# The memory read-out of an attention kernel done head by head: two 64-row matmuls into two PSUM banks in place of one 128-row matmul

## The chip, the core and the metric

The program runs on one core of one Trainium2 chip. The metric is the time of one execution on the device, in microseconds (us); lower is better. The chip's engines run side by side, each with its own queue of instructions in program order: TensorE (PE: weight loads, called PEld in the trace, and matmuls), VectorE (DVE), ScalarE (ACT), GpSimd (POOL) and SyncE (SP), which only issues transfers here.

## The reference

Four batches, eight heads, 576 tokens and head size 64 go through causal softmax attention mixed with a compressive memory, then through two MLPs (512 to 2048 to 512):

```python
B, H, S, D = q.shape                      # 4, 8, 576, 64
a = softmax(causal(q @ k.T / sqrt(D)))
local = a @ v
q_p = elu(q) + 1
mem_ret  = einsum('bhsd,bhde->bhse', q_p, M_prev)
mem_norm = einsum('bhsd,bhd->bhs', q_p, z_prev)[..., None] + 1e-06
g = sigmoid(beta)
x = g * mem_ret / mem_norm + (1 - g) * local    # (tokens, 512)
x = silu(x @ w_in) @ w_out                      # first MLP
h = x @ w_in2;  out = (h * tanh(softplus(h))) @ w_out2
```

The change is in how `mem_ret` and `mem_norm` reach the mix.

## The kernel before

Heads are taken in pairs: head 0 of a pair lies on partitions 0 to 63, head 1 on partitions 64 to 127 (16 pairs). A step is one block of up to 128 queries of one pair: first 32 steps with query blocks 0 and 1 of all pairs, then 48 with blocks 2, 3 and 4 (block 4 has 64 queries), 80 steps in all. Each step goes through three stages:

- `stage_a` makes the scores of both heads in two PSUM banks, the softmax numerators as two f16 parts (high and low), and sends them through a transposing DMA. For the blocks 0 and 1 the scores are f32 matmuls on 64 rows (partitions), one for each head; then masks are added by a matmul with the identity on 128 rows.
- `stage_b` is the read-out. On PE it multiplies the transposed numerators by v, three f16 matmuls for each head and key block (65, 64 and 65 columns; column 65 of v is ones and gives the softmax denominator). Then comes one f32 matmul for the memory: the features of both heads (`er`, 128 rows) against a block-diagonal matrix `rm` of 128 rows and 130 columns, in which each head has its 64 columns of M_prev, one of z_prev, and zeros in the other head's rows. After the last step of a pair of query blocks (or after block 4) DVE adds the small constants to the denominators, takes reciprocals, multiplies by the gates (`gvv`) and by the numerators (`t4`), and POOL adds memory and local part (`x`).
- `stage_c` transposes `x` on PE (line 610), ACT or DVE copies it out of PSUM (`xo`), and SP stores it to the scratch tensor `xd` in DRAM, from which `chunk_x` loads the MLP's inputs, 256 tokens at a time.

The mix of a pair of query blocks lies in banks 6 and 7: an even block in bank 6, an odd one in bank 7, each with columns 0 to 64 for the local part of head 0, 65 to 129 for that of head 1, and 130 to 259 for the memory of both. The transposes of `stage_c` go to columns 260 and up of the same two banks.

All instructions are handed to a planner (`Plan`) as operations with a priority, the regions that they write and read, and a cost formula. `issue` then runs a list scheduler over all engines and so fixes the order of every queue before the program is built. Regions are kept as one interval of bytes: a strided view that spans banks 6 and 7 counts as everything from its first to its last byte. Attention has a higher priority than the MLP's matmuls (`gemm1`, `gemm2`), which fill PE in between. On PE a line number says little, since nearly all matmuls are issued by the helper `mm` (line 375); `tt` is line 328, `stt` 322, `ts` 319, `act` and `copy` on ACT 314, and DMAs are line 385.

In the first part of the program the first MLP's weights are unpacked (`weight_unit`, 16 units), measured (`weight_scale`, once for the first eight units, which are w_in, and once for the last eight, w_out) and split into two f16 parts (`weight_split`) on ACT and DVE, while attention runs beside it. `hidden` of the first MLP needs the scale of w_out as well. Matmul outputs of `gemm1` go to banks 2 and 3 in turn, so the third group of eight (`gemm1` of step 2) waits until `hidden` of step 0 has read bank 2.

Of the kernel before, what the change touches and what calls it, by code (L numbers as in the profile page):

```python
# [9 lines left out]
F32 = mybir.dt.float32  # L10
F32R = mybir.dt.float32r
U32 = mybir.dt.uint32
# [3 lines left out]
ALU = mybir.AluOpType  # L16
# [16 lines left out]
PT_BLOCKS = 50  # L33
VM = 130 + NQ * 2 * (D + 1)
COLD = 50000.
# [143 lines left out]
def attn_moe_moe2_kernel(ctx: ExitStack, tc: tile.TileContext, kq, vm, beta, w1, w2, out):  # L179
# [92 lines left out]
    pt_tile, = carve([PT_BLOCKS, 128], F16)  # L272
    kqr, rmr, rvr = ring(carve([2, S], F32, 2)), ring(carve([130], F32, 3)), ring(carve([VM - 130], F32, 2))
    khr, klr = ring(carve([S], F32R, 2)), ring(carve([S], F32R, 2))
# [119 lines left out]
    def setup():  # L394
# [9 lines left out]
        def consts():  # L404
# [7 lines left out]
            make_identity(nc, ident)  # L412
            nc.gpsimd.memset(eps[:, 0:2], 1e-9 * PSCALE)
            nc.gpsimd.memset(eps[:, 2:4], 1e-6)
            nc.gpsimd.memset(ones, 1.0)
            nc.gpsimd.memset(onesf, 1.0)
            for t in scales:
                nc.gpsimd.memset(t[:, 2:4], 1.0)
            for t in v1s:
# [4 lines left out]
        g3 = gb.rearrange("p (a h) -> p a h", h=2)  # L424
        ts(p, gv[:, :, 0:2], g3, -0.5, ALU.mult, 0.5, ALU.add)
        ts(p, gv[:, :, 2:4], g3, 0.5, ALU.mult, 0.5, ALU.add)

# [15 lines left out]
    def load_vm(v, prio):  # L443
        p, _, nk = VISITS[v]
        n = nk * 2 * (D + 1)
        t, rm[v] = rvr()[:, 0:n], rmr()
        rv[v] = t.rearrange("p (n e d) -> p n e d", n=nk, e=2)
        dma(prio, t, vm[p, :, 130:130 + n], reads=[])
        dma(prio, rm[v], vm[p, :, 0:130], reads=[])

# [23 lines left out]
    def prep_v(v, prio):  # L474
# [7 lines left out]
        mm(prio, [(total, ones, top, True, True)])  # L482
        ts(prio, inv[:, 0:2], total.to_broadcast([128, 2]), 2.0**-14, ALU.mult, 1e-30, ALU.max)
        ts(prio, inv[:, 0:2].bitcast(U32), inv[:, 0:2].bitcast(U32), 0x7F800000, ALU.bitwise_and)
        other(prio, "DVE", 160, lambda: nc.vector.reciprocal(out=scale, in_=inv[:, 0:1]), [scale], [inv])
# [80 lines left out]
    def stage_b(n, prio):  # L566
# [4 lines left out]
        v1, v2, gvv = vv[v]  # L571
        vb = bank[6 + qt % 2]
        if qt < 4:
# [16 lines left out]
        g = banks[0:R, 512 * 6:512 * 8].rearrange("p (b c) -> p b c", b=2)[:, 0:m, 0:260].rearrange("p b (a c) -> p b a c", a=4)  # L590
        den, t4, x = denr()[0:R, 0:m], t4r()[0:R, 0:m], xr()[0:R, 0:m]
        each = lambda y: y[0:R].unsqueeze(1).to_broadcast([R, m, 4])
        tt(prio, den, g[:, :, :, D], each(eps), ALU.add)
        other(prio, "DVE", 165, lambda: nc.vector.reciprocal(out=den, in_=den), [den], [den])
        tt(prio, den, den, each(gvv), ALU.mult)
        tt(prio, t4, g[:, :, :, 0:D], den.unsqueeze(3).to_broadcast([R, m, 4, D]), ALU.mult)
        tt(prio, x, t4[:, :, 0:2], t4[:, :, 2:4], ALU.add, ("POOL", "DVE"))
        xts[n] = (x, R)
# [319 lines left out]
```

## Time and profile before

| | |
|---|---|
| median of 3 runs | 1025.33 us (1025.13 to 1026.48) |
| the profiled execution: its own time | 1025.4 us |
| its span (first to last instruction) | 1023.6 us |
| PE matmuls busy | 948.2 us, 93% of the span |
| DVE, ACT, POOL busy | 673.4, 642.5, 273.9 us |
| TensorE's granted clock, mean over the span | 0.96 |

The profiled execution takes 1.8 us more than its span, and lies 0.1 us above the median of the runs. Busy times of engines overlap. A PE row's duration holds a fixed latency, so matmuls that follow each other overlap in it; what a matmul costs in a full queue is the distance between its start and the start of the next one.

### The profile page before, as it was taken

To read this page: it belongs to the slowest core of one execution; us is meant where nothing else is said; L and a number is where in the kernel's file an instruction comes from. 1 tells how busy PE (TensorE), PEld (TensorE's weight loads), DVE (VectorE), ACT (ScalarE), POOL (GpSimd) and SP (SyncE) were. 2 spreads that over 40 slices of the span, in tenths; PEclk is the share of its full clock that TensorE was granted. 3 is DMA by queue.
4 is the path that set the end of the run, shared out by engine and by line. 5 is a ranking of instruction groups with operands and counts; after the bars stand their busy time and mean duration, and the time that the engine had idled before them with its cause. 6 is when DMAs were issued, how large, how long until landed. Compare 5 with 4: busy or idle time off the path is not lost.

```text
span 1023.6 us, 20794 instructions
## 1 busy us (share of the span) xinstructions
PE 948.2 (93%) x8364; PEld 732.2 (72%) x8364; DVE 673.4 (66%) x1231; ACT 642.5 (63%) x1095; POOL 273.9 (27%) x280
## 2 busy tenths in 40 slices
PE   2436589999999999999999999999999999999998
PEld 1225478888888888888888888766676766766665
DVE  6988687787787878777757756754544545544433
ACT  7977665666666756756667676744555545555544
POOL 1110123343343433432322522212212122222221
PEclk9956589999999999999999999999999999999999
DMA  9767924775787767845353341100100101000000
GB/s 322 230 148 208 228 58 114 162 187 133 183 156 150 151 137 148 176 114 130 105 199 104 104 146 61 42 30 14 42 22 21 32 12 42 22 21 22 1 21 21
DMA packets 149904, 107.93 MB, mean 105 GB/s; under 512 B 111152, under 2 KB 139312, under 8 KB 145712
## 3 DMA queue, kind: packets, MB, share of 16 engines
q1 hardware_dynamic: 149664, 106.60, 40.1%
q8 instruction: 65, 1.06, 0.4%
q14 instruction: 31, 0.25, 0.1%
q10 hardware_dynamic: 144, 0.00, 0.0%
HBM read 66.21 MB, written 14.16 MB: 79 GB/s over the span
## 4 chain that ended last, share of the span: by engine, by line
PE 85%; DMA 6%; DVE 4%; ACT 4%; issue 1%; SPq 0%; POOL 0%; DVEq 0%; POOLq 0%; ACTq 0%
PE banks L375 84%; DMA arena<-arena 2%; DVE w L322 1%; PE banks L610 1%; DMA g<-w 1%; ACT w L314 1%; DMA xs<-xd 1%; ACT arena L314 1%; DMA ws<-w 1%; DVE arena L322 1%; DMA arena<-kq 1%; ACT ws L671 0%; DVE w L328 0%; DVE arena L328 0%; DMA arena<-vm 0%
## 5 line engine op out<-in xcount | busy, mean ns | idle before, releaser
L375 PEld LDWEIGHTS <-w 128*128 128x128 f16 x3456 | 334.8, 98 | 43.3 <-issue 4.2
L375 PEld LDWEIGHTS <-arena 128*128 128x128 f16 (+1 forms) x3168 | 225.5, 101 | 80.1 <-DMA arena<-arena 27.5
L328 POOL TENSOR_TENSOR g<-ga,g 128x512 f16<-128x512 f32 x108 | 144.1, 1335 | 345.7 <-ACT g L314 327.4
L375 PE MATMUL banks<-xh,w 128*128 128x256 f16 x1728 | 213.8, 275 | 2.6 <-DVE ga L322 2.6
L375 PE MATMUL banks<-g,w 128*128 128x256 f16 x1728 | 209.8, 273 | 0.1
L375 PE MATMUL banks<-xh,arena 128*128 128x256 f16 x1728 | 198.6, 273 | 0.0
L375 PE MATMUL banks<-arena,g 128*128 128x512 f16 x864 | 197.4, 379 | 0.0
L375 PE MATMUL banks<-arena 128*128 128x65 f16 (+6 forms) x1728 | 119.0, 235 | 62.1 <-DMA arena<-arena 24.1
L375 PEld LDWEIGHTS <-g 128*128 128x128 f16 x864 | 84.5, 98 | 87.6
L314 ACT ACTIVATE ga<-ga 128x512 f32<-128x512 f32 x108 | 67.6, 628 | 77.5 <-DVE ga L319 53.6
L314 ACT ACTIVATE arena<-arena 128x256 f32<-128x256 f32 (+6 forms) x180 | 101.5, 592 | 18.5 <-PE banks L375 9.5
L322 DVE SCALAR_TENSOR_TENSOR ga<-ga,banks 128x512 f32<-128x512 f32 x108 | 73.7, 683 | 54.2 <-ACT ga L314 53.7
L322 DVE SCALAR_TENSOR_TENSOR arena<-arena 128x256 f16<-128x256 f32 (+6 forms) x144 | 106.1, 746 | 3.9 <-ACT arena L314 3.4
L314 ACT ACTIVATE w<-w 128x512 f32<-128x512 f32 x108 | 66.6, 625 | 47.3 <-DVE w L319 26.3
L314 ACT ACTIVATE arena<-banks,arena 128x128 f32<-128x128 f32 (+4 forms) x144 | 73.9, 545 | 33.9 <-DVE arena L546 25.9
L314 ACT ACTIVATE g<-ga 128x512 f16<-128x512 f32 x106 | 66.3, 626 | 28.7 <-DVE ga L322 28.2
L328 POOL TENSOR_TENSOR arena<-arena 128x256 f32<-128x256 f32 (+1 forms) x48 | 44.0, 916 | 139.1 <-DVE arena L328 89.3
L314 ACT ACTIVATE ga<-banks,xsc 128x512 f32<-128x512 f32 x72 | 49.2, 685 | 49.2 <-PE banks L375 45.5
L546 DVE TENSOR_REDUCE arena<-banks 128x2 f32<-128x256 f32 (+3 forms) x80 | 64.3, 804 | 23.8 <-PE banks L375 19.9
L328 POOL TENSOR_TENSOR g<-w,g 128x512 f16<-128x512 f32 x36 | 41.6, 1156 | 126.2 <-ACT g L314 126.2
L375 PEld LDWEIGHTS banks<-arena 128*128 128x128 f32 (+2 forms) x288 | 42.4, 228 | 32.9 <-ACT arena L314 29.6
L319 DVE TENSOR_SCALAR ga<-banks,xsc 128x512 f32<-128x512 f32 x36 | 27.0, 750 | 51.7 <-PE banks L375 51.6
(95 smaller groups left out, 942.0 us busy)
## 6 DMA issues: line engine op xcount, KB each, us to landing
ws<-w SPq DMA_DIRECT2D x28, 1024.0 KB, 5.3
arena<-kq SPq DMA_DIRECT2D x16, 576.0 KB, 5.0
arena<-vm SPq DMA_DIRECT2D x16, 325.0 KB, 3.4
xs<-xd SPq DMA_DIRECT2D x9, 512.0 KB, 4.6
yd<-w SPq DMA_DIRECT2D x36, 128.0 KB, 1.9
xs<-yd SPq DMA_DIRECT2D x9, 512.0 KB, 3.8
arena<-kq SPq DMA_DIRECT2D x16, 256.0 KB, 3.4
xd<-arena SPq DMA_DIRECT2D x32, 128.0 KB, 2.5
```

The costliest lines, as they stand in the source:

```text
L314: return ("ACT", ns, lambda: nc.scalar.activation(out=out, in_=in_, func=func, scale=scale, bias=bias))
L319: return ("DVE", ns, lambda: nc.vector.tensor_scalar(out=out, in0=in0, scalar1=s1, scalar2=s2, op0=op0, **kw))
L322: return ("DVE", 1.04 * cols(out) + 160, lambda: nc.vector.scalar_tensor_tensor(out=out, in0=in0, scalar=s, in1=in1, op0=op0, op1=op1))
L328: return (e, ns, lambda: eng.tensor_tensor(out=out, in0=in0, in1=in1, op=op))
L375: nc.tensor.matmul(out=o, lhsT=l, rhs=r, start=a, stop=z)
L546: other(prio, "DVE", 1.04 * cols(both) + 146, lambda: nc.vector.tensor_reduce(out=m1, in_=both, axis=AX, op=ALU.max, negate=True), [m1], [ ...
L610: plan.add(prio, [("PE", 56, lambda o=o, x2=x2: nc.tensor.transpose(o, x2, ident[0:R, 0:R]))], [o], [x2, ident], edge=(107, 56))
```

## The change

`rm` holds 65 columns in place of 130: for each partition the 64 values of its own head's M_prev and one of z_prev, without the zeros. The memory part becomes two f32 matmuls, one for each head, on that head's 64 partitions and with 65 columns. The mix is laid out by head: head 0 in bank 6, head 1 in bank 7, an even query block at columns 0 to 129 and an odd one at 130 to 259, each with 65 columns of the local part and then 65 of the memory. The constants, gates and the tiles of the mix change their order to match; the number of their instructions and elements stays. The planner and its cost formulas stay.

```diff
-VM = 130 + NQ * 2 * (D + 1)
+VM = D + 1 + NQ * 2 * (D + 1)
...
-        dma(prio, rm[v], vm[p, :, 0:130], reads=[])
+        dma(prio, rm[v], vm[p, :, 0:D + 1], reads=[])
...
-        vb = bank[6 + qt % 2]
+        c0 = 130 * (qt % 2)
...
-            o = vb[0:R, 65 * e:65 * e + 65]
+            o = bank[6 + e][0:R, c0:c0 + 65]
...
-        mm(prio, ms + [(vb[0:R, 130:260], er[v][:, 128 * qt:128 * qt + R], rm[v], True, True)])
+        for e in range(2):
+            r = slice(64 * e, 64 * e + 64)
+            ms.append((bank[6 + e][0:R, c0 + 65:c0 + 130], er[v][r, 128 * qt:128 * qt + R], rm[v][r], True, True))
+        mm(prio, ms)
...
-        g = banks[0:R, 512 * 6:512 * 8].rearrange("p (b c) -> p b c", b=2)[:, 0:m, 0:260].rearrange("p b (a c) -> p b a c", a=4)
+        g = banks[0:R, 512 * 6:512 * 8].rearrange("p (e c) -> p e c", e=2)[:, :, 0:130 * m].rearrange("p e (a c) -> p e a c", c=65)
...
-        tt(prio, x, t4[:, :, 0:2], t4[:, :, 2:4], ALU.add, ("POOL", "DVE"))
+        t4 = t4.rearrange("p e (q k) d -> p e q k d", k=2)
+        tt(prio, x.rearrange("p q e d -> p e q d"), t4[:, :, :, 0], t4[:, :, :, 1], ALU.add, ("POOL", "DVE"))
...
-    mz = np.zeros((NP, 2, D, 2, D + 1), f32)
-    for e in range(2):
-        mz[:, e, :, e, :D] = np.asarray(M_prev).reshape(NP, 2, D, D)[:, e]
-        mz[:, e, :, e, D] = np.asarray(z_prev).reshape(NP, 2, D)[:, e]
+    mz = np.concatenate([np.asarray(M_prev).reshape(NP, 128, D), np.asarray(z_prev).reshape(NP, 128, 1)], 2)
```

Since each step now writes both banks, the planner orders all queues differently from the first read-outs on. Three places follow.

The first is PE, at the read-outs of the steps 2 and 3 (an even and an odd block). "128x130" is the memory matmul before; a "128x65" without a LDWEIGHTS row ahead of it is one of the two after (an f32 matmul loads its own weights). L610 (L616 after) are the transposes of `stage_c` of the pair ahead of it, diag the matmul of `weight_scale`. Before:

```order
L375 MATMUL banks<-arena_98 128x65
L375 MATMUL banks<-arena_98 128x130 [waits DMAHW2_49]
L610 MATMUL banks<-ident_66,arena_98 128x128 [waits Pool_49]
L610 MATMUL banks<-ident_66,arena_98 128x128
L375 MATMUL banks<-diag_81,onesf_96 128x128 [waits DVE_49]
L375 LDWEIGHTS arena_98 [waits DMAHW2_49]
L375 MATMUL banks<-arena_98 128x65 [waits Activation_49]
```

After:

```order
L616 MATMUL banks<-ident_66,arena_98 128x128 [waits Pool_49]
L616 MATMUL banks<-ident_66,arena_98 128x128
L375 MATMUL banks<-diag_81,onesf_96 128x128 [waits DVE_49]
L375 LDWEIGHTS arena_98 [waits DMAHW0_49]
L375 MATMUL banks<-arena_98 128x65 [waits Activation_49]
...
L375 MATMUL banks<-arena_98 128x65
L375 MATMUL banks<-arena_98 128x65 [waits DMAHW2_49]
L375 MATMUL banks<-arena_98 128x65
```

Before, the even block's read-out (first two rows) stood ahead of the transposes and only the odd block's waited for ACT, which copies the transposes out of PSUM; after, the even block's read-out stands behind them and has that wait.

The second place is PE just ahead of `gemm1` of step 2 (the first `xh_75,w_73` row). L610 and L616 are `stage_c` of the pair of steps 14 and 15, the `ones` matmul is `prep_v`'s, 128x256 with the two masks is `stage_a` of step 19. Before, with the read-out of step 16 just above the first row:

```order
L375 MATMUL banks<-arena_98 128x130
L610 MATMUL banks<-ident_66,arena_98 128x128 x2
L375 LDWEIGHTS ones_72
L375 MATMUL banks<-arena_98,ones_72 128x1
L375 MATMUL banks<-arena_98 128x256 x2
L375 LDWEIGHTS ident_0_67
L375 MATMUL banks<-mask_68,ident_0_67 128x128
...
L375 LDWEIGHTS w_73
L375 MATMUL banks<-xh_75,w_73 128x256
```

After:

```order
L375 LDWEIGHTS ones_72
L375 MATMUL banks<-arena_98,ones_72 128x1
L616 MATMUL banks<-ident_66,arena_98 128x128 x2
L375 LDWEIGHTS w_73
L375 MATMUL banks<-xh_75,w_73 128x256
...
L375 MATMUL banks<-xh_75,w_73 128x256
L375 LDWEIGHTS arena_98
L375 MATMUL banks<-arena_98 128x65
```

The read-out of step 16 and the scores of step 19 have moved from ahead of this group of `gemm1` to behind it.

The third place is DVE, between the scale of w_out (`wsc`, `cvec`) and the first `hidden` (the row with `ga_79`). The `xsc` row makes the factor that `hidden` needs; `banks,arena` 128x512 is the `t4` product of steps 14 and 15; L546 and L479 are reductions of `stage_a` and `prep_v`. Before:

```order
L328 TENSOR_TENSOR arena_98<-banks,arena_98 128x512
...
L322 SCALAR_TENSOR_TENSOR arena_98<-arena_98 128x256
L641 RECIPROCAL wsc_0_92<-cvec_0_94 128x1
L546 TENSOR_REDUCE arena_98<-banks 128x2
L479 TENSOR_REDUCE arena_98<-arena_98 128x1
...
L322 SCALAR_TENSOR_TENSOR arena_98<-arena_98 128x256
L328 TENSOR_TENSOR xsc_89<-cvec_0_94,xsc_89 128x2
...
L546 TENSOR_REDUCE arena_98<-banks 128x2
L322 SCALAR_TENSOR_TENSOR w_73<-w_73,wsc_0_92 128x1024
L322 SCALAR_TENSOR_TENSOR ga_79<-ga_79,banks 128x512
```

After:

```order
L328 TENSOR_TENSOR arena_98<-banks,eps_71 128x8
...
L647 RECIPROCAL wsc_0_92<-cvec_0_94 128x1
L328 TENSOR_TENSOR cvec_0_94<-cvec_0_94 128x1
L319 TENSOR_SCALAR wsc_0_92<-wsc_0_92 128x1
L328 TENSOR_TENSOR xsc_89<-cvec_0_94,xsc_89 128x2
L328 TENSOR_TENSOR arena_98<-banks,arena_98 128x512
L322 SCALAR_TENSOR_TENSOR arena_98<-arena_98 128x256
L546 TENSOR_REDUCE arena_98<-banks 128x2
L319 TENSOR_SCALAR arena_98<-banks 128x2
L322 SCALAR_TENSOR_TENSOR w_73<-w_73,wsc_0_92 128x1024
L322 SCALAR_TENSOR_TENSOR ga_79<-ga_79,banks 128x512
```

The `t4` product, a split of `prep_v`, two reductions and one more operation have moved from ahead of the `xsc` row to behind it or further down, and the reduction over the scores of step 19, the last one ahead of the weight split before, stands there no longer.

## Rows read from the trace of the kernel before

**Rows 1.** Busy time, share of the span and instructions of each engine.

```profile
PE 948.2 (93%) x8364; PEld 732.2 (72%) x8364; DVE 673.4 (66%) x1231; ACT 642.5 (63%) x1095; POOL 273.9 (27%) x280
```

**Rows 2.** Windows: stretch, length, busy time by engine, PE clock, DMA share, GB/s.

```profile
core 0: us, PE busy (x) PEld busy (x) DVE busy (x) ACT busy (x) POOL busy (x), PEclk, DMA share, GB/s
0.00:131.50 131.50, 62.02 (x385) 41.95 (x386) 106.43 (x228) 102.22 (x181) 14.27 (x41) 0.71 0.77 224
131.50:1023.60 892.10, 886.19 (x7979) 690.26 (x7978) 566.98 (x1005) 540.33 (x915) 259.62 (x239) 1.00 0.35 88
```

**Rows 3.** Memory matmuls by shape after 131.5: count, busy us, mean ns, idle.

```profile
L375 PE MATMUL banks<-arena 128*128 128x130 f32 x94 | 22.0, 315 | 0.0
...
L375 PE MATMUL banks<-arena 128*64 128x130 f32 x32 | 6.6, 288 | 0.0
```

**Rows 4.** Timeline, PE: memory matmul of 128 queries, then of 64 (start, us).

```profile
187.60 0.47 PE L375 MATMUL banks<-arena 128*128 128x130 f32 x2
187.91 0.27 PE L375 MATMUL banks<-xh,w 128*128 128x256 f16 x1
...
249.09 0.41 PE L375 MATMUL banks<-arena 128*64 128x130 f32 x2
249.44 0.28 PE L375 MATMUL banks<-xh,w 128*128 128x256 f16 x1
```

**Rows 5.** Timeline, PE: twelve MLP matmuls in a row.

```profile
312.83 1.48 PE L375 MATMUL banks<-xh,w 128*128 128x256 f16 x12
```

**Rows 6.** Timeline, PE: 64-row f32 scores, with what precedes and follows.

```profile
184.05 0.27 PE L375 MATMUL banks<-g,w 128*128 128x256 f16 x1
184.25 0.38 PE L375 MATMUL banks<-arena 64*128 64x128 f32 x2
...
184.47 0.28 PE L375 MATMUL banks<-arena 64*128 64x128 f32 x2
184.68 0.23 PE L375 MATMUL banks<-mask,ident 128*128 128x128 bf16 x1
...
172.07 0.38 PE L375 MATMUL banks<-arena 64*128 64x256 f32 x2
172.39 0.23 PE L375 MATMUL banks<-mask,ident 128*128 128x128 bf16 x1
```

**Rows 7.** Timeline, weight loads of the scores' second pass at 184 us.

```profile
184.36 0.19 PEld L375 LDWEIGHTS banks<-arena 64*128 64x128 f32 x2
```

**Rows 8.** Timeline, PE: the wait ahead of step 2's matmuls; two moved stages.

```profile
131.59 0.80 PE L375 MATMUL banks<-xh,w 128*128 128x256 f16 x3 [2.65 <-DVE ga L322]
...
156.28 0.65 PE L375 MATMUL banks<-arena 128*128 128x65 f16 x8
156.77 0.82 PE L375 MATMUL banks<-g,w 128*128 128x256 f16 x6
...
154.21 0.70 PE L375 MATMUL banks<-arena 64*128 64x256 f32 x4
```

**Rows 9.** Timeline, DVE, from the scale of w_out to the first split.

```profile
124.99 0.69 DVE L328 TENSOR_TENSOR arena<-banks,arena 128x512 f32<-128x512 f32 x1
...
125.65 0.48 DVE L322 SCALAR_TENSOR_TENSOR arena<-arena 128x256 f16<-128x256 f32 x1
...
126.44 0.41 DVE L479 TENSOR_REDUCE arena<-arena 128x1 bf16<-128x256 f32 x1
...
126.89 0.42 DVE L322 SCALAR_TENSOR_TENSOR arena<-arena 128x256 f32<-128x256 f32 x1
...
129.06 0.69 DVE L546 TENSOR_REDUCE arena<-banks 128x2 f32<-128x512 f32 x1 [1.16 <-PE banks L375]
```

**Rows 10.** Timeline, PE: the read-out of step 4, an even block.

```profile
48.08 1.08 PE L375 MATMUL banks<-arena 128*128 128x65 f16 x8 [2.46 <-DVE arena L328]
```

**Rows 11.** Timeline, SP: store of x, load of the first MLP inputs.

```profile
75.69 0.53 SPq L385 DMA_DIRECT2D xd<-arena  x1
79.75 0.39 SPq L385 DMA_DIRECT2D xs<-xd  x1
```

**Rows 12.** Waits of PE in the first 131.5 us: total, times, longest.

```profile
PE banks L375 <- DMA arena<-arena: 24.1, 4, 12.5
```

More of the change, by code (lines that the diff above doesn't have):

```diff
@@ L412, in consts @@
             make_identity(nc, ident)
-            nc.gpsimd.memset(eps[:, 0:2], 1e-9 * PSCALE)
-            nc.gpsimd.memset(eps[:, 2:4], 1e-6)
+            nc.gpsimd.memset(eps[:, 0:4:2], 1e-9 * PSCALE)
+            nc.gpsimd.memset(eps[:, 1:4:2], 1e-6)
             nc.gpsimd.memset(ones, 1.0)
@@ L417, in consts @@
             for t in scales:
-                nc.gpsimd.memset(t[:, 2:4], 1.0)
+                nc.gpsimd.memset(t[:, 1:4:2], 1.0)
             for t in v1s:
@@ L424, in setup @@
         g3 = gb.rearrange("p (a h) -> p a h", h=2)
-        ts(p, gv[:, :, 0:2], g3, -0.5, ALU.mult, 0.5, ALU.add)
-        ts(p, gv[:, :, 2:4], g3, 0.5, ALU.mult, 0.5, ALU.add)
+        ts(p, gv[:, :, 0:4:2], g3, -0.5, ALU.mult, 0.5, ALU.add)
+        ts(p, gv[:, :, 1:4:2], g3, 0.5, ALU.mult, 0.5, ALU.add)
     rq, rk, rv, rm, kk, vv, qq, er = {}, {}, {}, {}, {}, {}, {}, {}
@@ L447, in load_vm @@
         rv[v] = t.rearrange("p (n e d) -> p n e d", n=nk, e=2)
-        dma(prio, t, vm[p, :, 130:130 + n], reads=[])
-        dma(prio, rm[v], vm[p, :, 0:130], reads=[])
+        dma(prio, t, vm[p, :, D + 1:D + 1 + n], reads=[])
+        dma(prio, rm[v], vm[p, :, 0:D + 1], reads=[])
     def prep_q(v, j, prio):
@@ L482, in prep_v @@
         mm(prio, [(total, ones, top, True, True)])
-        ts(prio, inv[:, 0:2], total.to_broadcast([128, 2]), 2.0**-14, ALU.mult, 1e-30, ALU.max)
-        ts(prio, inv[:, 0:2].bitcast(U32), inv[:, 0:2].bitcast(U32), 0x7F800000, ALU.bitwise_and)
+        ts(prio, inv[:, 0:4:2], total.to_broadcast([128, 2]), 2.0**-14, ALU.mult, 1e-30, ALU.max)
+        ts(prio, inv[:, 0:4:2].bitcast(U32), inv[:, 0:4:2].bitcast(U32), 0x7F800000, ALU.bitwise_and)
         other(prio, "DVE", 160, lambda: nc.vector.reciprocal(out=scale, in_=inv[:, 0:1]), [scale], [inv])
@@ L589, in stage_b @@
         m = 1 + qt % 2
-        g = banks[0:R, 512 * 6:512 * 8].rearrange("p (b c) -> p b c", b=2)[:, 0:m, 0:260].rearrange("p b (a c) -> p b a c", a=4)
-        den, t4, x = denr()[0:R, 0:m], t4r()[0:R, 0:m], xr()[0:R, 0:m]
-        each = lambda y: y[0:R].unsqueeze(1).to_broadcast([R, m, 4])
-        tt(prio, den, g[:, :, :, D], each(eps), ALU.add)
+        g = banks[0:R, 512 * 6:512 * 8].rearrange("p (e c) -> p e c", e=2)[:, :, 0:130 * m].rearrange("p e (a c) -> p e a c", c=65)
+        den, t4, x = denr()[0:R, :, 0:2 * m], t4r()[0:R, :, 0:2 * m], xr()[0:R, 0:m]
+        quad = lambda y: y.rearrange("p e (q k) -> p e q k", k=2)
+        each = lambda y: y[0:R].rearrange("p (e k) -> p e k", e=2).unsqueeze(2).to_broadcast([R, 2, m, 2])
+        tt(prio, quad(den), quad(g[:, :, :, D]), each(eps), ALU.add)
         other(prio, "DVE", 165, lambda: nc.vector.reciprocal(out=den, in_=den), [den], [den])
-        tt(prio, den, den, each(gvv), ALU.mult)
-        tt(prio, t4, g[:, :, :, 0:D], den.unsqueeze(3).to_broadcast([R, m, 4, D]), ALU.mult)
-        tt(prio, x, t4[:, :, 0:2], t4[:, :, 2:4], ALU.add, ("POOL", "DVE"))
+        tt(prio, quad(den), quad(den), each(gvv), ALU.mult)
+        tt(prio, t4, g[:, :, :, 0:D], den.unsqueeze(3).to_broadcast([R, 2, 2 * m, D]), ALU.mult)
+        t4 = t4.rearrange("p e (q k) d -> p e q k d", k=2)
+        tt(prio, x.rearrange("p q e d -> p e q d"), t4[:, :, :, 0], t4[:, :, :, 1], ALU.add, ("POOL", "DVE"))
         xts[n] = (x, R)
@@ L903 @@
         "kq": np.concatenate([pair_t(np.asarray(k)), pair_t(np.asarray(q))], 2),
-        "vm": np.concatenate([mz.reshape(NP, 128, 130), vp.reshape(NP, 128, NQ * 2 * (D + 1))], 2),
+        "vm": np.concatenate([mz, vp.reshape(NP, 128, NQ * 2 * (D + 1))], 2),
         "betar": np.ascontiguousarray(np.broadcast_to(np.asarray(beta), (128, H))),
```

2 lines of the change are left out of this document (1 added, 1 removed).

## The prediction

> **What bounds the kernel now.** The page's first part says that PE is busy for 93% of the span [rows 1], but that is an average over two stages, so I looked at windows next. In the first 131.5 us PE works for 62.0 us at a mean granted clock of 0.71, and DVE and ACT, which unpack weights and do the softmax, for 106.4 and 102.2; from 131.5 to the end PE is busy for 886.2 of 892.1 us at full clock [rows 2]. So there are two currencies. After 131.5 every nanosecond that PE's queue gains or loses is a nanosecond of the result, and nothing else matters as long as PE isn't made to wait. Before 131.5 PE's own time is nearly free, and what counts is when the queue becomes full for good, which the first wait on the list of PE's waits (24.1 us on transposing DMAs, the longest 12.5) shows to be a matter of chains through several engines [rows 12].
>
> The boundary itself is one wait: PE reaches `gemm1` of step 2 and stands for 2.65 us until DVE has done `hidden` of step 0 [rows 8].
>
> **The memory matmul, full steps.** An f32 matmul makes two passes, each with its own weight load. Before, from the start of the first pass to the start of the next instruction, it holds PE for 187.60 to 187.91 = 0.31 us [rows 4]. Two 64-row f32 matmuls on different banks stand in this trace already: the scores of blocks 0 and 1. They show four things.
> - Entry. In a row of MLP matmuls starts are (1.48 - 0.27) / 11 = 0.11 us apart [rows 5]; from such a matmul to the first 64-row one it is 184.05 to 184.25 = 0.20 [rows 6]. Going over to 64 rows costs 0.09: PE empties first.
> - Overlap. The first passes of both heads are two rows in 0.38 us, about the length of one, so the heads do run side by side (some 0.01 apart) [rows 6].
> - Pass. First to second pass is 184.25 to 184.47 = 0.21 to 0.22, with 128 columns [rows 6].
> - Exit. From the second pass to the next 128-row instruction it is 0.21 with 128 columns and 0.32 with 256 [rows 6]: 0.11 for each 128 columns and 0.10 besides. With 65 columns that makes 0.05 + 0.10 = 0.15.
>
> What no row shows is the pass with 65 columns. If columns paced it, it would shrink to 0.05 + 0.10 = 0.16. If the weight loads pace it, it stays at 0.21, since the weights are still 128 query columns. The loads of the second pass begin at 184.36, 0.11 after the first, and their matmul starts 0.11 after that [rows 6, 7]: at 128 columns load and columns take equally long, so the load alone is enough to hold the pass at 0.21. I take 0.21 and keep 0.16 as the lower end.
>
> The Trainium skill (TensorE: Matmul & The Clock Gate, the section on LDWEIGHTS) says that a weight load's time goes with its columns and not with its rows, about 107 ns for 128 columns; as an estimate by it, two loads make a pass of 0.214 us. The 0.11 between the loads agrees, and it speaks against this change: half the rows, and no shorter load.
>
> After: 0.09 + 0.21 + 0.01 + 0.15 = 0.46 us, against 0.31: +0.15 a step (+0.10 at the lower end). Of the f32 rows 94 lie after 131.5, two passes each, so 47 steps [rows 3]; step 16 comes to them (below): 48 x 0.15 = **+7.2 us** (lower end +4.8). The order of the changed kernel's PE has a 64-row stretch of scores directly behind a read-out in four places only, and often the next read-out's 128-row f16 matmuls directly behind one, so nearly each pays both ways.
>
> **The memory matmul, block 4.** There are 16 (32 rows [rows 3]). Before, 249.09 to 249.44 = 0.35 [rows 4], in which PE already goes over from 64 output columns back to 128. After, there is one more change of shape ahead of it (0 to 0.09), the load has 64 columns, so the pass shrinks to between 0.10 and 0.21, and the exit is 0.15: 0.26 to 0.46, or -0.09 to +0.11 a step, -1.4 to +1.8 in all. With 0.09, 0.10 and 0.15 and the 0.01 it is 0.35: **0**.
>
> **Moved into the full stretch.** The read-out of step 16 (0.49 at full clock, 156.28 to 156.77) and the scores of step 19 (0.70) [rows 8] did their work on PE inside the wait for `hidden`; now they stand behind `gemm1` of step 2, which waits at the head of the queue. **+1.2 us**.
>
> **The boundary comes earlier.** The row of DVE that ends the wait stands behind the first split of w_out. Ahead of that split, three operations leave: a reduction of 0.41, a `prep_phi` operation of 0.42, and the reduction over the scores of step 19, 0.69, for which DVE had first waited 1.16 on PE [rows 9]. The other moves there are within the stretch (the `t4` product of 0.69 and the 0.48 of `prep_v` go behind the `xsc` row, so ACT can start its tanh sooner). 0.41 + 0.42 + 1.16 + 0.69 = **-2.7 us**; if ACT is late instead, 0.
>
> **Earlier waits.** An even block's read-out now stands behind the transposes of the pair ahead and waits for their copy on ACT; its 1.08 us at half clock [rows 10] no longer lies in that wait but ahead of the odd block's. The first MLP input needs three such pairs (steps 2 to 7): 0 to +3.2. Against it, SP stores x at 75.69 and then stands until 79.75, when it may load the first MLP input, 4.06 us in which nothing behind it goes out [rows 11]; in the new order two loads and a transposing DMA have moved into that gap. 0 to -4.1. The two have no row that nets them, and I take **0**.
>
> **Costs taken as nothing.** The DVE operations of the mix keep their counts and elements, and DVE has 566.98 us of work in the 892 [rows 2]; POOL's addition gets shorter inner runs, and POOL works 259.62 us there. Their results are wanted only by transposes that stand further back in PE's queue; if one were late, PE's whole queue would stand behind that transpose. The loads of `rm` stay as many, with half the bytes, in a stretch where DMA queues are busy 0.35.
>
> **Sum.** 7.2 + 0 + 1.2 - 2.7 + 0 = +5.7 on the profiled execution's 1025.4 (span 1023.6, and 0.1 over the median of the runs): **1031.1 us**. Of this kernel about 0.2%, 2.05 us, can be told from no change, so "same" is 1023.3 to 1027.4.
>
> **Rivals.**
> A, *the early part gives it back*: transposing DMAs that leave SP up to 4.1 us sooner shorten the first stretch by as much. 1031.1 - 4.1 = 1027.0, and 1024.6 with the short pass as well. For it: the chain of the first stretch runs through such transfers [rows 12]. Against it: the last of them before the boundary stands in the same place in both orders. 0.14, counted as same.
> B, *the early part loses*: the even read-outs' +3.2 stands on the chain and `hidden` isn't sooner (ACT late): 1031.1 + 3.2 + 2.7 = 1037.0. 0.13.
> C, *the change of shape costs nothing*, and the result is on the other side: if PE drew the weights of the 64-row matmuls in while the f16 ones ran, a step would take 0.21 + 0.01 + 0.05 = 0.27, 0.04 less than before, 1.9 in all, and with the early -1.5 the time is 1022.0, faster. With that -1.5 it decides once both changes of shape together cost under 0.03 us a step. Against it stands each entry and exit in rows 6, 0.09 and 0.10. 0.06.
> The Trainium skill (TensorEngine Tiling, Theoretical Speedup) promises up to twice the speed for a contraction of 64 or less. As an estimate by it, 0.31 / 2 over 48 steps and 0.35 / 2 over 16 would save 10.2 us, and with the early -1.5 the time would be 1013.7. The same page (Key Properties) says that a change of tiling mode drains the engine, and this trace sides with that: 0.20 against 0.11.
> D, *the heads run one after the other*: 0.21 + 0.05 = 0.26 more in each of 64 steps, 16.6 us: 1047.7. The paired scores speak against it. 0.04.
>
> **How the numbers follow.** The forecast has 0.63, with its own range from 1028 (short pass) to 1034. Slower by over 0.2%: the forecast, B and D, 0.80. Within 0.2%: A, 0.13 of it. Faster: C and the rest of A, 0.07. The range leaves out C, D, the lowest of A and about half of B: **1025.5 to 1036.5**.
>
> **What would show it.** After: f32 rows of 64 rows and 65 columns, two starts about 0.01 apart and a second pair 0.21 later; 0.12 from the last f16 matmul to the first of them and 0.15 from the last to the next 128-row start; the first matmul of `gemm1` of step 2 near 131.59 - 2.7 = 128.9 us, and PE without idle time behind it. A second pass at 0.16 makes the time 1028.7. I am wrong if the entry isn't paid, if PE waits behind the boundary (a transpose on POOL's addition), or if the boundary moves by more than 4 us.

## The result, and the profile after

The changed kernel takes 1034.35 us (median of 4 runs, 1032.40 to 1036.38) where the kernel before takes 1025.88 beside it (4 runs, 1025.13 to 1026.48): ratio 1.0083, 95% interval 1.0061 to 1.0105, some 8.5 us slower. The profiled execution took 1033.64 us, its span is 1031.8, so 8.2 us more than before.

PE's busy time in the first part of the page answers to [rows 1]:

```profile
PE 957.9 (93%) x8524; PEld 735.5 (71%) x8524; DVE 662.2 (64%) x1224; ACT 644.7 (62%) x1102; POOL 268.2 (26%) x280
```

The windows, cut at the first matmul of `gemm1` of step 2 as in [rows 2]; columns as there:

```profile
0.00:124.60 124.60, 61.86 (x403) 41.08 (x404) 105.16 (x223) 101.55 (x181) 14.62 (x40) 0.94 0.78 229
124.60:1031.80 907.20, 896.00 (x8121) 694.46 (x8120) 557.09 (x1003) 543.11 (x923) 253.56 (x240) 1.00 0.35 86
```

Read two things. The cut has moved from 131.59 to 124.66 us, 6.9 earlier. What follows it has grown from 892.1 to 907.2 us, and in that stretch PE is no longer busy all the time: 11.2 us are missing from 907.20, where before 5.9 were missing from 892.10. -6.9 + 15.1 = +8.2: the loss is entirely behind the cut, and nearly half of it is hidden by a gain ahead of it.

**The read-out.** The timeline of PE over one step of the changed kernel (start, duration, count), which answers to [rows 4] and [rows 6]. Each row was cut so that a pass begins with it, so the second row's four matmuls include the third row's two:

```profile
303.53 0.25 PE L375 MATMUL banks<-arena 128*128 128x65 f16 x3
...
303.71 0.44 PE L375 MATMUL banks<-arena 64*128 64x65 f32 x4
...
303.88 0.28 PE L375 MATMUL banks<-arena 64*128 64x65 f32 x2
304.09 0.28 PE L375 MATMUL banks<-xh,w 128*128 128x256 f16 x1
```

The f16 matmuls start 0.03 apart, so the last of the three starts at 303.59. From there: entry 0.12, pass 0.16 (303.71 to 303.88), exit 0.20 (303.88 to 304.09; the two heads are 0.007 apart within a pass). The starts in the trace to the nanosecond, as medians over the 18 steps that are followed by an MLP matmul: 0.121, 0.007, 0.154, 0.006, 0.204, and 0.119 in place of 0.109 for the matmul behind. From the last f16 start to the next 128-row start a full step holds PE for 0.493 us; before it was 0.333 (0.029, 0.192, 0.112). A step of block 4 went from 0.376 to 0.390 (means of the 16).

**The cut.** The last reduction over the maxima of w_out, and what came next on DVE. Before:

```profile
118.31 0.15 DVE L331 TENSOR_REDUCE mx<-topw 128x1 f32<-128x8 f32 x1
122.61 0.16 DVE L319 TENSOR_SCALAR arena<-banks 128x2 f32<-128x2 f32 x1 [4.15 <-PE banks L375]
122.68 0.28 DVE L328 TENSOR_TENSOR diag<-ident,mx 128x128 f32<-128x128 f32 x1
```

After:

```profile
116.85 0.15 DVE L331 TENSOR_REDUCE mx<-topw 128x1 f32<-128x8 f32 x1
116.92 0.16 DVE L319 TENSOR_SCALAR arena<-arena 128x2 uint32<-128x2 uint32 x1
117.04 0.29 DVE L328 TENSOR_TENSOR diag<-ident,mx 128x128 f32<-128x128 f32 x1
```

Before, a row of `prep_v` that reads bank 7 stood ahead of the scale's `diag` and waited 4.15 us, until the read-out of step 15, which writes bank 7 and stands ahead of it in the program, was through. In the new order no such row is in the way, and `diag` is 5.6 us earlier. The read-out of step 15 itself is 4.0 us earlier too, at 117.10 where it was at 121.14: its transposing DMA leaves SP only 0.39 us sooner (113.95 for 114.34) but lands at 117.05 for 121.09.

**The end of the first MLP.** PE's waits from 480 to 660 us (total, times, longest); before there is none in this stretch:

```profile
PE banks L375 <- DVE diag L328: 2.2, 2, 1.5
PE banks L375 <- DVE ga L322: 2.0, 2, 1.0
PE banks L375 <- POOL g L328: 0.9, 1, 0.9
PE banks L375 <- DVE xh L322: 0.9, 1, 0.9
PE banks L375 <- DVE arena L328: 0.8, 1, 0.8
PE banks L375 <- ACT w L314: 0.4, 1, 0.4
```

The window from 625 to 660 us (second column: PE busy), before and then after:

```profile
625.00:660.00 35.00, 35.00 (x303) 29.44 (x301) 26.46 (x49) 26.44 (x39) 8.80 (x7) 1.00 0.10 31
```

```profile
625.00:660.00 35.00, 29.72 (x265) 25.82 (x263) 24.80 (x42) 24.68 (x34) 4.82 (x4) 1.00 0.18 61
```

The timeline tells why. Before, the second MLP's `gemm1` (weights in `arena`) is there while the first MLP still runs, and each fills the other's waits:

```profile
636.90 4.42 PE L375 MATMUL banks<-xh,arena 128*128 128x256 f16 x39
641.16 1.47 PE L375 MATMUL banks<-g,w 128*128 128x256 f16 x12
```

After, the first MLP's last matmuls (`g,w`) wait by themselves, and `gemm1` of the second comes when they are over:

```profile
645.36 0.49 PE L375 MATMUL banks<-diag,onesf 128*128 128x128 f32 x2 [1.54 <-DVE diag L328]
645.82 0.38 PE L375 MATMUL banks<-g,w 128*128 128x256 f16 x2
647.11 2.56 PE L375 MATMUL banks<-g,w 128*128 128x256 f16 x22 [0.92 <-POOL g L328]
649.51 0.27 PE L375 MATMUL banks<-xh,arena 128*128 128x256 f16 x1
```

The second MLP's split weights lie over the attention's buffers (`w_second` is carved from the same arena), so most of its units can't be unpacked until attention is through. The last read-out moved from 497.8 to 517.6 us; behind it lay 148.8 us of first MLP before (to 646.5), and 131.8 after (to 649.4). From the last read-out to the first matmul of the second MLP it takes 139.1 and 132.0. Before, the first MLP lasted longer than that chain; after, it runs out. e2, e4 and e11 below bear out that the late end of attention is the cause.

### The profile page after: what moved, and what is told of

Read it like the earlier page. It is cut to its first block, busy times and chain, and to the rows that moved or that the text cites. A ratio compares the mean times of both kernels' runs of the same rounds, so it can differ in the third digit from the quotient of the medians.

```text
span 1031.8 us, 21093 instructions
## 1 busy us (share of the span) xinstructions
PE 957.9 (93%) x8524; PEld 735.5 (71%) x8524; DVE 662.2 (64%) x1224; ACT 644.7 (62%) x1102; POOL 268.2 (26%) x280
## 4 chain that ended last, share of the span: by engine, by line
PE 85%; ACT 5%; DVE 4%; DMA 4%; issue 1%; SPq 0%; POOL 0%; DVEq 0%; ACTq 0%; POOLq 0%
PE banks L375 84%; DMA ws<-w 2%; ACT arena L314 1%; DVE w L322 1%; ACT ws L677 1%; ACT w L314 1%; DMA g<-w 1%; PE banks L616 1%; DVE arena L322 1%; ACT ws L314 1%; DVE arena L328 1%; DMA yd<-w 0%; DMA arena<-arena 0%; DVE w L328 0%; DVE arena L319 0%
## 5 line engine op out<-in xcount | busy, mean ns | idle before, releaser
L375 PEld LDWEIGHTS <-arena 128*128 128x128 f16 (+1 forms) x3168 | 223.2, 101 | 54.9 <-DMA arena<-arena 13.7
L328 POOL TENSOR_TENSOR g<-ga,g 128x512 f16<-128x512 f32 x108 | 133.7, 1239 | 315.6 <-ACT g L314 291.8
L375 PE MATMUL banks<-arena 128*64 128x65 f16 (+6 forms) x1888 | 121.1, 238 | 36.5 <-ACT arena L314 22.7
L314 ACT ACTIVATE arena<-arena 128x256 f32<-128x256 f32 (+6 forms) x186 | 105.7, 597 | 16.8 <-PE banks L375 12.8
L546 DVE TENSOR_REDUCE arena<-banks 128x2 f32<-128x256 f32 (+3 forms) x80 | 64.4, 805 | 28.8 <-PE banks L375 26.8
L328 POOL TENSOR_TENSOR arena<-arena 128x256 f32<-128x256 f32 (+1 forms) x48 | 48.3, 1007 | 131.9 <-DVE arena L328 98.8
L319 DVE TENSOR_SCALAR w<-banks,xsc 128x512 f32<-128x512 f32 x36 | 27.0, 751 | 81.7 <-PE banks L375 81.7
L375 PEld LDWEIGHTS banks<-arena 64*128 64x128 f32 (+1 forms) x448 | 41.8, 213 | 41.6 <-ACT arena L314 32.3
```

The source lines that it names most:

```text
L314: return ("ACT", ns, lambda: nc.scalar.activation(out=out, in_=in_, func=func, scale=scale, bias=bias))
L319: return ("DVE", ns, lambda: nc.vector.tensor_scalar(out=out, in0=in0, scalar1=s1, scalar2=s2, op0=op0, **kw))
L328: return (e, ns, lambda: eng.tensor_tensor(out=out, in0=in0, in1=in1, op=op))
L375: nc.tensor.matmul(out=o, lhsT=l, rhs=r, start=a, stop=z)
L546: other(prio, "DVE", 1.04 * cols(both) + 146, lambda: nc.vector.tensor_reduce(out=m1, in_=both, axis=AX, op=ALU.max, negate=True), [m1], [ ...
```

## The experiments

Three theories. **S**: the change of shape costs PE at each entry and exit. **O**: the planner's other order, which follows from the new layout, gives the early cut and takes it back at the end of the first MLP. **R**, the rival to S: the loss is the order's.

Most kernels have the order of issue fixed, so that one thing changes at a time: the list scheduler gives way to a table of the operations and engines that it had chosen (both kernels have the same 5194 operations):

```diff
     def issue(self):
-        ...
+        for k, e in ORDER:
+            next(f for x, _, f, _ in self.ops[k][1] if x == e)()
```

All results in one table. "Cut" is the first matmul of `gemm1` of step 2 in the profiled execution, "rest" is from there to the end of its span. Ratios are against the kernel before on the same chip (its medians there were 1024.13 to 1025.88).

| kernel | median us | ratio, 95% interval | cut | rest |
|---|---|---|---|---|
| before | 1025.88 | | 131.6 | 892.0 |
| changed | 1034.35 | 1.0083, 1.0061 to 1.0105 | 124.7 | 907.2 |
| e1_old_order | 1031.43 | 1.0050, 1.0033 to 1.0066 | 131.4 | 897.6 |
| e2_new_order | 1024.73 | 0.9995, 0.9983 to 1.0007 | 123.9 | 898.5 |
| e3_mixed_order | 1019.64 | 0.9936, 0.9922 to 0.9949 | 125.3 | 894.1 |
| e4_regions | 1034.54 | 1.0088, 1.0073 to 1.0102 | 132.9 | 899.7 |
| e5_full_rows | 1037.37 | 1.0113, 1.0094 to 1.0132 | 129.1 | 907.5 |
| e6_paired | 1027.08 | 1.0014, 0.9995 to 1.0032 | 123.6 | 903.3 |
| e7_apart | 1065.97 | 1.0401, 1.0375 to 1.0428 | 129.7 | 934.7 |
| e8_scale_first | 1021.02 | 0.9959, 0.9944 to 0.9974 | 132.4 | 890.0 |
| e9_changed_mixed | 1026.37 | 1.0015, 1.0004 to 1.0026 | 124.4 | 900.5 |
| e10_with_scores | 1053.13 | 1.0283, 1.0262 to 1.0304 | 124.4 | 926.4 |
| e11_regions_mixed | 1027.55 | 1.0020, 1.0010 to 1.0030 | 123.8 | 902.0 |

### e1_old_order: the read-out alone

The changed kernel, `ORDER` that of the kernel before.

> The changed kernel, its instructions issued in the order of the kernel before on every engine (a table of the planner's choices replaces the planner). Theory S and O together (S: the change between matmuls of 128 and of 64 rows costs PE about 0.16 us in each of 48 full read-outs, 8.7 us in all; O: the planner's other order brings gemm1 of step 2 about 6.9 us forward and costs about 6 us of stalls at the first MLP's end): the order's two effects go, S stays: 1025.9 + 7.5 to 8.7 = 1033.4 to 1034.6 us, the first matmul of gemm1 of step 2 back at about 131.6 us, hardly a PE stall after 480 us. Rival R, the loss is the order's: 1025 to 1028 us.

Measured 1031.43, the cut at 131.4. R falls: the order is as it was, and 0.50% are still lost. But the loss is 5.6 us in the rest and not 7.5 to 8.7. The reason is in the rows: in the old order 14 of the 47 full steps are followed by 64-row matmuls (7 by scores, 7 by the transposes of block 4), and those pay no full exit, as here, from the second pass at 315.23 to the scores at 315.31:

```profile
315.07 0.44 PE L423 MATMUL banks<-arena 64*128 64x65 f32 x4
...
315.23 0.28 PE L423 MATMUL banks<-arena 64*128 64x65 f32 x2
315.31 0.48 PE L423 MATMUL banks<-arena_r 64*128 64x512 f32 x2
```

Such a step takes 0.37 to 0.40 us, against 0.43 in the kernel before, which changes shape there too: it gets cheaper. So the read-out's price depends on the order: +5.6 us in the old one (0.6 of it a wait behind one step), +8.1 in the new one, where every full step pays both ways (48 steps: 15.99 us in e2, 23.85 in the changed kernel; 16 of block 4: 6.04 and 6.24).

### e2_new_order: the order alone

The kernel before, `ORDER` that of the changed kernel.

> The kernel before, its instructions issued in the order of the changed kernel on every engine. S and O: the order alone is worth -6.9 + 1 + 5.5 to 6, so 1025 to 1026.5 us; gemm1 of step 2 begins near 124.7 us, PE stalls about 9 us after 480 us, and the first matmul of the second MLP comes at about 640 us. Rival L, attention ends late in the changed kernel because its read-outs are longer and not because of the order: the early start is kept and the stalls are not there, 1020 us. Rival R: about 1034 us.

Measured 1024.73, no difference that counts and 0.3 us below the expected range: the cut comes 7.7 us earlier and the rest is 6.4 us longer. Waits at the end of the first MLP are there without any 64-row read-out, 4.8 us on the list where about 9 were expected. PE's waits from 480 to 660 us and the window from 625:

```profile
PE banks L423 <- DVE diag L376: 2.2, 2, 1.5
PE banks L423 <- DVE ga L370: 1.7, 2, 1.1
PE banks L423 <- POOL g L376: 0.9, 1, 0.9
```

```profile
625.00:660.00 35.00, 32.55 (x255) 25.61 (x253) 26.71 (x51) 24.95 (x36) 6.63 (x6) 0.95 0.12 36
```

Those are three of the six rows of the changed kernel's list, which come to 7.2 us. Rival L (attention is late because its read-outs are longer) falls. Part of the 6.4 is TensorE's clock: the same 22 matmuls behind the wait on POOL that take 2.56 us in the changed kernel take 4.21 here.

```profile
636.82 4.21 PE L423 MATMUL banks<-g,w 128*128 128x256 f16 x22 [0.92 <-POOL g L376]
```

The mean granted clock from 636.80 to 641.00 is 0.59 (1.00 over the same matmuls in the changed kernel), so most of this stretch ran at the lower of the two levels, 1.2 GHz.

### e3_mixed_order: the early half without the late half

The kernel before, in the new order up to the cut and in its own from there.

> The kernel before, issued in the order of the changed kernel up to the first matmul of gemm1 of step 2, and from there in its own order. S and O: the early start of 6.9 us is kept, about 1 us is given back for the read-outs that stand behind it, and the stalls at the first MLP's end are not there: 1019 to 1020.5 us, faster than the kernel before. Rival G, what is gained by then is waited for later in the old order: 1024 to 1026 us.

Measured 1019.64, ratio 0.9936: 6 us faster than the kernel before and the fastest of all kernels here. The early cut is kept (125.3), the rest is 2.1 us longer than before, and rival G falls. PE has no wait of over 0.4 us behind the cut.

### e4_regions and e11_regions_mixed: the planner told the two banks apart

The new false dependences come from regions that are one interval over both banks. Here the planner gets one region to a bank:

```diff
-        tt(prio, quad(den), quad(g[:, :, :, D]), each(eps), ALU.add)
+        per = [bank[6 + e][0:R, 0:130 * m] for e in range(2)]
+        tt(prio, quad(den), quad(g[:, :, :, D]), each(eps), ALU.add, reads=per + [eps])
...
-             banks[:, 512 * 6:512 * 8].rearrange("p (b c) -> p b c", b=2)[:, 0:m, 260:260 + R])
+             banks[:, 512 * 6:512 * 8].rearrange("p (b c) -> p b c", b=2)[:, 0:m, 260:260 + R],
+             reads=[bank[6 + i][:, 260:260 + R] for i in range(m)])
```

> The changed kernel, with the planner told the two banks apart: the copy out of the transposes and the reads of the mix are entered as one region to a bank and not as one stretch from bank 6 to bank 7, so that the read-out of an even block no longer waits for the copy of the pair before. The planner is free, and its own plan ends attention 15 us earlier. S and O: the stalls at the first MLP's end shrink from 9 to about 3 us, gemm1 of step 2 stays near 124.7 us, the read-outs stay as dear: 1027.5 to 1030 us. Rival, the stalls come from elsewhere than the late end of attention: 1033 to 1035 us.

Measured 1034.54: no gain, and the time is the rival's. The mechanism is not. The rest is 7.5 us shorter than in the changed kernel, the last read-out comes 377.7 us behind the cut (366.2 before, 392.9 in the changed kernel, 384.3 in e2), and the window at the end of the first MLP is full again:

```profile
625.00:660.00 35.00, 35.00 (x323) 31.40 (x321) 26.15 (x46) 25.18 (x35) 6.15 (x5) 1.00 0.09 30
```

What I had not foreseen is that the planner's new order loses the early cut (132.9), as much as it wins. e11 puts the two halves together: the changed kernel's order up to the cut, that of e4 behind it.

> The changed kernel in its own order up to the first matmul of gemm1 of step 2, and from there in the order that the planner made with the two banks told apart. If that order lost only the early start (gemm1 of step 2 at 132.9 us instead of 124.7) and did take the stalls away (7.2 us less from gemm1 of step 2 to the last matmul): 1034.5 - 8.2 = 1026.3 us, 1025 to 1028. Rival, the two go together, an early start makes the late stalls whatever the order behind it: 1032 to 1035 us.

Measured 1027.55, the cut at 123.8, as expected: the early gain and the late loss are separate effects of one scheduler. The last read-out comes 379.8 us behind the cut, and the window from 625 to 660 us is full here as well.

### e5_full_rows: the layout without the change of shape

One head to a bank as in the changed kernel and in its order, but 128 rows, with zeros in the other head's rows:

```diff
-            r = slice(64 * e, 64 * e + 64)
-            ms.append((bank[6 + e][0:R, c0 + 65:c0 + 130], er[v][r, 128 * qt:128 * qt + R], rm[v][r], True, True))
+            ms.append((bank[6 + e][0:R, c0 + 65:c0 + 130], er[v][:, 128 * qt:128 * qt + R], rm[v][:, 65 * e:65 * e + 65], True, True))
```

> The changed kernel in its own order, one head to a bank as before, but each head's memory product as a matmul of 128 rows and 65 columns on a matrix padded with zeros: no change of shape, four passes in a row instead of two pairs. S: the entry falls from 0.121 to about 0.03 us and no exit of 0.204 us stands behind the last pass; four passes of at least 0.11 us and at most the 0.19 us of a pass of 130 columns give 0.47 to 0.79 us a step against 0.49: 1033 to 1048 us. Rival B, entry and exit belong to the two banks and not to the rows: 0.121 and 0.204 us stay, at least 0.65 us a step, 1042 to 1056 us.

Four passes in one step on PE's timeline, cut as above:

```profile
285.71 0.63 PE L423 MATMUL banks<-arena 128*128 128x65 f32 x4
...
285.85 0.50 PE L423 MATMUL banks<-arena 128*128 128x65 f32 x3
...
286.07 0.28 PE L423 MATMUL banks<-arena 128*128 128x65 f32 x1
286.18 0.38 PE L423 MATMUL banks<-g,w 128*128 128x256 f16 x2
```

The entry is 0.029 (the last f16 matmul starts at 285.681 in the trace), the passes 0.14, 0.11, 0.11, and 0.11 to the next matmul: no exit. Entry and exit don't belong to the two banks, and rival B falls; in the full steps they come with the change of rows. A change of columns alone costs an exit too: in block 4 of this kernel (128 rows, 64 columns of weights) the passes come every 0.058 to 0.061 us, and the next matmul with 128 columns 0.152 behind the last. Half the columns halve the pass, so on full rows it is the loaded columns that pace it and not the 65 that stream. A step takes 0.502 us against 0.493, so twice the passes at full rows cost as much as half of them with two changes of shape; the rest is 0.4 us longer (907.53 against 907.16), which is 48 times that difference. The medians differ by 3.0 us; what is not in the rest lies ahead of the cut, which comes 4.4 us later in the profile, and was not taken apart.

### e6_paired and e7_apart: half the changes of shape, and twice

e6 (the diff) moves the products of an even block to those of the odd one; e7 puts each head's product behind that head's f16 matmuls. Both keep the changed kernel's order.

```diff
-        for e in range(2):
-            r = slice(64 * e, 64 * e + 64)
-            ms.append((bank[6 + e][0:R, c0 + 65:c0 + 130], er[v][r, 128 * qt:128 * qt + R], rm[v][r], True, True))
+        for q in range(qt - qt % 2, qt + 1) if last(n) else ():
+            for e in range(2):
+                r, c = slice(64 * e, 64 * e + 64), 130 * (q % 2) + 65
+                ms.append((bank[6 + e][0:R, c:c + 65], er[v][r, 128 * q:128 * q + R], rm[v][r], True, True))
```

> The changed kernel in its own order, the memory products of an even block moved behind those of the odd block of its pair: one stretch of 64-row matmuls to a pair instead of two. S, a cost for each change of shape: a pair's 2 x 0.486 = 0.97 us becomes 0.121 + 3 x 0.155 + 0.204 = 0.79, 0.18 us less in 24 pairs: 4.3 us faster than the changed kernel, 1029.5 to 1031 us. Rival P, a cost for each 64-row product whatever stands beside it: 1033.5 to 1035 us.

> The changed kernel in its own order, each head's memory product straight behind the f16 matmuls of that head: two stretches of 64-row matmuls to a step instead of one. S: 2 x (0.121 + 0.155 + 0.204) = 0.96 us against 0.486, 0.47 us more in 48 steps and half of that or less in the 16 of block 4: 1057 to 1063 us. Rival P, only that the two heads no longer stand side by side, two more passes of 0.155 us: 1049 to 1054 us.

A pair's stretch in e6, four passes of both heads:

```profile
209.61 0.66 PE L423 MATMUL banks<-arena 64*128 64x65 f32 x8
...
209.77 0.50 PE L423 MATMUL banks<-arena 64*128 64x65 f32 x6
...
209.99 0.28 PE L423 MATMUL banks<-arena 64*128 64x65 f32 x2
210.20 0.28 PE L423 MATMUL banks<-xh,w 128*128 128x256 f16 x1
```

The first pass takes 0.16, the next two 0.11 each, the exit again 0.20: 0.716 us for two steps instead of 2 x 0.493. In 24 pairs and block 4 the read-outs take 23.4 us where the changed kernel's take 30.1: 6.6 us less, against the 4.3 that S gave with a later pass at 0.155. The rest is only 3.9 us shorter, since this profiled execution has the slow stretch of e2 (22 matmuls in 4.17 us instead of 2.56) and waits as long as the changed kernel. The median is 7.3 us lower, below S's range, with runs from 1025.13 to 1032.70. In e7 one head alone:

```profile
203.02 0.43 PE L423 MATMUL banks<-arena 64*128 64x65 f32 x2
...
203.18 0.27 PE L423 MATMUL banks<-arena 64*128 64x65 f32 x1
203.39 0.28 PE L423 MATMUL banks<-xh,w 128*128 128x256 f16 x1
```

0.487 us for one head, against 0.493 for both at once. The rest is 27.5 us longer, which alone would give 1061.9 us, within S's range, although the 16 steps of block 4 pay more than I gave them: 0.38 for each head, 0.77 against 0.39 for both. The measured 1065.97 lies beyond the range because the cut comes 5.0 us later, which S had left out and which was not taken apart. P falls on both sides: the price goes with the changes of shape.

### e8_scale_first: what held the cut

The kernel before in its own order, but thirteen operations (the scale of w_out and `hidden` of step 0) are issued just ahead of the read-out of step 15:

```diff
-ORDER = [...]
+i = position of the read-out of step 15
+ORDER = ORDER[:i] + scale_of_w_out + xsc + hidden_0 + the rest
```

> The kernel before in its own order, but for thirteen operations: the scale of w_out and the hidden of step 0 (on DVE, PE and ACT) are issued ahead of the read-out of step 15 instead of behind it. Theory W: in the kernel before they stand behind a row of DVE that waits 4.15 us for that read-out, which waits 3.81 us for its transposing DMA. With them ahead, gemm1 of step 2 has no wait for hidden left and comes when PE's own queue is through, 2.65 us and the 0.7 us of the diag matmul earlier: near 128.2 us, and 1022 to 1023 us in all. Rival V, the early start of the changed kernel comes from other transfers and read-outs alone: 131 to 132 us, 1025.5 us.

Measured 1021.02 against 1024.13 on the same chip, ratio 0.9959: V falls and W holds; the time is 1 us below the expected range. In its profiled execution (at 1024.18 us the slowest of its six runs) the last unit of w_out came late, so its cut can't be set beside 131.59. Its last Square on ACT, and the cut, now without a wait:

```profile
121.52 1.11 ACT L719 ACTIVATE ws<-w 128x1024 f32<-128x1024 f32 x1
```

```profile
132.41 1.83 PE L423 MATMUL banks<-xh,w 128*128 128x256 f16 x8
```

From that Square to the cut it is 10.9 us. In the kernel before the same Square starts at 116.61, 15.0 ahead of the cut, and in the changed kernel at 115.49, 9.2 ahead. So of the 6.9 us, 1.1 come from the weights being through sooner and about 4.1 from what e8 moves. The remaining 1.7 are a difference and not shown by a run; the read-out and scores that stand behind `gemm1` in the new order would be their likely source.

### e9_changed_mixed: do the parts add up

The changed kernel in the order of e3.

> The changed kernel in the mixed order: its own up to the first matmul of gemm1 of step 2, from there that of the kernel before. If the read-out's price and the two effects of the order simply add up: 1031.4 (changed kernel in the old order) - 5.9 (what the mixed order gave the kernel before) = 1025.5 us, 1024.5 to 1026.5. Rival, the later read-outs make the old order wait: 1028 us or more.

Measured 1026.37, 1.0015 times before. They add up: the changed read-out costs this order 6.4 us in the rest (900.5 against e3's 894.1).

### e10_with_scores: the products in a stretch that is there anyway

If the price is the change of shape, the products should stand next to the 64-row scores. A step's products go to the head of the scores of the step three later:

```diff
+            owed.append((bank[6 + e][0:R, c0 + 65:c0 + 130], er[v][r, 128 * qt:128 * qt + R], rm[v][r], True, True))
...
-            mm(prio, [x for y in zip(*ms) for x in y] + masks)
+            mm(prio, owed + [x for y in zip(*ms) for x in y] + masks)
+            owed.clear()
```

> The changed kernel in the mixed order, with the memory products of a step (from step 17 on, blocks 0 to 3) put at the head of the 64-row scores of the step three later, so that they stand in a stretch of 64-row matmuls that is there anyway; operations that depend on them are issued as late as that makes them. S: the product then costs two passes of 0.11 us and no change of shape of its own, 0.22 us against the 0.30 of the 128-row form and the 0.46 of the changed kernel: 1019.6 - 45 x 0.08 + 0.2 for block 4 = 1016 to 1017 us. Rival, the mix comes later and PE waits for it at the transposes: 1020 to 1026 us. Rival P, a 64-row product costs the same wherever it stands: about 1025.5 us.

Measured 1053.13, and the expectation failed, worse than its rival. The products do run as S says (0.16 for the first pass and 0.08 to the scores, as in e1's rows), but the mix comes later and PE waits. The largest rows of its list from 125 us on:

```profile
PE banks L423 <- ACT arena L362: 11.5, 22, 1.3
PE banks L674 <- POOL arena L376: 4.2, 7, 1.2
PE banks L423 <- DVE arena L376: 3.4, 4, 1.6
```

With the six smaller rows PE waits for 24.4 us there. An order made for this form was not tried, so whether the 64-row form can win beside the scores stays open.

## Why the prediction was right, and where it was wrong

The direction came out, and the size lies within the range (1031.1 forecast, 1034.35 measured), but the size did so in part by luck. The read-out's sum is right because two of its steps failed by the same 0.05 us in opposite directions. The early gain was 4.2 us larger than forecast, and behind the cut 15.1 us came where 8.4 were forecast; these two largely cancel as well. Two of the prediction's own signs of being wrong came true: the boundary moved by more than 4 us, and PE waits behind it, though not at a transpose.

- **Entry, 0.09.** Right: 0.121 against 0.029 to the first pass before, so 0.092, and 0.029 again in e5 without the change of shape.
- **Overlap.** Right: heads 0.007 us apart; D falls. e7 sharpens it: a lone head's pass takes 0.161, as both do together.
- **Pass, 0.21.** Wrong: 0.161, the lower end. The step that failed is "so the load alone is enough to hold the pass at 0.21": with 65 columns for the 128 of [rows 6] the pass did shrink. e6 shows that later passes of both heads come every 0.11 us with the same 128 query columns to load, and its weight loads of the two heads start 0.006 us apart: they run side by side. Only the first pass of a stretch takes 0.05 more. By the formula of the Trainium skill (TensorE: Matmul & The Clock Gate, the section on LDWEIGHTS) one load of 128 columns takes 107 ns, as an estimate; the 0.111 of e6 agrees.
- **Exit, 0.05 + 0.10.** Wrong: 0.204. The step "0.11 for each 128 columns and 0.10 besides" took the streamed columns to pace it down to 65; [rows 6] already had 0.21 at 128 columns, and it stays there. The 0.11 is the pass that the 128 loaded columns hold in a row, and 0.204 - 0.111 = 0.093 the change of shape, as much as the entry. With block 4's 64 query columns the exit is 0.151: a pass of 0.058, as in e5, and the same 0.093.
- **Their sum.** Pass 0.05 too long and exit 0.05 too short: 0.092 + 0.161 + 0.007 + 0.204 = 0.464 measured for 0.46, +0.16 a step against 0.304, and 0.01 more for the matmul behind. In the new order the read-outs cost +8.1 us for +7.2; block 4, taken as 0, is +0.2 of it.
- **C, the change of shape costs nothing.** Fell, by entry and exit. Inside a stretch the halved rows do pay: two heads pass in 0.11 together in e6, and one after the other in 0.11 each in e5. The two changes of shape, 0.185 in a step, take that back. The Trainium skill (TensorEngine Tiling, Theoretical Speedup) promises up to twice the speed for a contraction of 64 or less; inside a stretch this trace agrees. The same page of the Trainium skill (TensorEngine Tiling, Key Properties) says that a change of tiling mode drains the engine; the trace agrees, with 0.093 each way.
- **The boundary, -2.7.** Right in sign, mis-sized: -6.9. The step that failed counted only operations that leave DVE's queue ahead of the split (0.41 + 0.42 + 1.16 + 0.69). It did not look further up, where a row of `prep_v` ahead of `diag` waited 4.15 us; e8 shows what stood behind that wait to be worth 3 to 4 us.
- **Moved, +1.2.** Not measured by itself. It was priced at full clock, but the granted clock is 0.51 from 124.60 to 130.50 us, and the moved read-out starts at 129.73.
- **"PE without idle time behind it".** Wrong. The prediction read the order at three places, all before 132 us, and took everything behind as hidden. e2 shows the new order alone to make PE wait at the end of the first MLP, e4 and e11 that another order hardly does (1.1 us in e4). The time in which PE isn't busy behind the cut grew by 11.2 - 5.9 = 5.3 us, most of the 15.1 - 8.1 = 7.0 us that are not the read-out's.
- **A and B.** B fell: the early part got faster. What the even blocks' waits cost by themselves no run shows. A's early size came true, -2.7 - 4.1 = -6.8 for -6.9, and a transposing DMA did land 4.0 us sooner, though it left SP only 0.39 sooner; how much of the gain that landing brings, beside what e8 moves, no run separates. What A didn't have is that the gain is given back.

## What to carry to other kernels

A short matmul on 64 rows between matmuls of 128 rows pays for both changes of shape, here 0.093 us each and 0.16 net on a product of 0.30. Half the rows do not shorten a pass as long as the loaded columns stay (0.111 for 0.112); the gain is that two heads share it. So such a matmul belongs in a stretch with others of its shape (e6), where that does not make others wait for it (e10). When a change touches what a scheduler sees as dependences, read the new order to the end of the program, above all where one phase hands its buffers to the next, and fix the order by a table before measuring the change itself. A wait far up in the queue of an engine that isn't the bottleneck can hold the start of the stage that is: e3 and e8 gained 6 and 3 us by order alone.

## What the runs showed of the hardware that was not expected

- A change of shape costs about 0.093 us each way beyond what the matmul ahead of it takes in a row: 0.121 - 0.029 on entry to 64 rows, 0.204 - 0.111 on exit to 128 rows, and the next f16 matmul then lasts 0.01 longer (0.119 to its successor for 0.109). The exit is no shorter with 65 columns than with the 128 of [rows 6]; with 64 columns of weights (block 4) it is 0.151. A change from 64 to 128 columns of weights on full rows has the same exit, 0.152 in e5. If 64-row matmuls follow there is none: it takes 0.077 us from the last start to the scores of the blocks 2 and 3, 0.105 to those of the blocks 0 and 1 and to the transposes of block 4 (all in e1).
- The first f32 pass of a stretch takes longer than the next: 0.161 and 0.111 on 64 rows, 0.14 and 0.11 on 128 rows with 65 columns, 0.192 and 0.112 with 130. Why is open.
- Behind waits of the same length the granted clock fell in two kernels and not in a third: 22 matmuls in 4.21 us in e2_new_order and 4.17 in e6_paired (granted clock 0.59 in both), in 2.56 us in the changed kernel (1.00), after 1.54 and 0.92 us of waiting in all three. What tells them apart is open.
